# Moving a batched FFT filter's transform between the matmuls of a gated feed-forward block

## The chip, the core and the metric

The kernel runs on one core of one Trainium2 chip. The metric is the device time of one execution in microseconds (us), the median of several runs. The engines spoken of are TensorE (PE, and PEld for its weight loads), VectorE (DVE), ScalarE (ACT), GpSimd (POOL) and SyncE (SP), whose queue issues the DMA transfers. PE writes its results to PSUM, of which there are eight banks of 128 x 512 float32 in this kernel's use; the others work in SBUF.

## What is computed

The input x is 8 batches of 3136 rows by 256 channels, in float32. A filter along the rows is applied by FFT, and a gated feed-forward block of width 1024 with a three-tap convolution along the rows follows.

```python
X = np.fft.rfft(x, axis=1)
y = np.fft.irfft(X * (filt_r + 1j * filt_i), n=3136, axis=1)
h = np.maximum(y @ w_in, 0.0)                     # 256 -> 1024
conv_out = sum(conv_w[k] * shifted(h, k - 1) for k in range(3))
out = (h * sigmoid(conv_out)) @ w_out             # 1024 -> 256
```

## The kernel before

**The transform.** 3136 is 112 x 28. The FFT, the filter and the inverse FFT are done as four stages of matmuls, each over 14 pieces per batch; a piece holds two of 28 columns or groups. Stage 1 (`first`, L323) multiplies x by tables `s1_sb`, and `store` (L313) copies the result from PSUM with ScalarE (L315) and sends it to a buffer `a_dram` in device memory. Stage 2 (`second`, L330) reads that buffer back in another order and multiplies it by `s2_sb`; `filt` (L340) applies the filter with three DVE instructions (L346 to L348) and one POOL sum (L350). Stage 3 (`third`, L353) multiplies by tables `i1_sb`, and `store` sends the result to `b_dram`. Stage 4 (`last_stage`, L210) reads that back and multiplies by `m2_sb`. Its result is the filtered y, written to SBUF by `last_out` (L219) as two tiles, a high part (`hi_act`, L146, ScalarE) and the remainder (`lo_dve`, L149, or `lo_pool`, L152). Because of the two trips through device memory, stage 2 of a batch needs all 14 pieces of its stage 1, and stage 4 all 14 of its stage 3.

**The forward part** (the loop at L375) runs stages 1 to 3 of all eight batches, one piece of each per iteration, with stage 1 some 18 iterations ahead of the rest (`SKEW`, L363). Tables and filter stay in SBUF. Stage 4 of batch 0 comes at its end (L416 to L422). The weights arrive as 64-bit floats and are converted to float32 in small steps by DVE, ACT and POOL (`convert_weights`, L279), also in this loop; PSUM is shared out as five banks under the name ps and three under pp.

**The gated layers** (the loop at L511) are 448 steps m. A step handles 448 rows and 128 of the 1024 hidden channels, in a software pipeline written out by hand: `inner` for step m (six matmuls into one bank `ps_h`), the projection `project` for step m-6 (three matmuls for each of four or three output tiles, into four banks `po`), then `relu` (two ScalarE instructions, L448 and L450) and `conv` (two DVE instructions, L455 and L456) for m-1, `gate` (sigmoid on ScalarE, L460, product on DVE, L461) for m-2, `split_g` (ScalarE and POOL) for m-3, and `evacuate`, which copies a finished `po` to SBUF by DVE (L496) in two of 16 steps. A `ps_h` bank comes free with the product L461. Stage 4 of batches 1 to 7 runs here: the dictionary `pieces` (L503) spreads its 98 pieces over the steps, two to three steps apart, leaving out steps of 16 named in `AVOID`; a piece takes one of the four `ps_h` banks, its matmuls stand between `inner` and `project`, and `last_out` stands near the end of the step. The order on PE, DVE, ACT and POOL is that of the program (`manual_schedule`).

Of the kernel before, what the change touches and what calls it, by code (L numbers as in the profile page):

```python
# [16 lines left out]
S = 3136  # L17
# [107 lines left out]
def tile_fft_filter_gated_ffn(  # L125
# [3 lines left out]
    fr: bass.AP,  # L129
    fi: bass.AP,  # L130
# [52 lines left out]
    b_dram = [dram.tile([N2, 112, D], F32, name=f"b_dram{b}") for b in range(B)]  # L183

    wc = ctx.enter_context(tc.tile_pool(name="wc", bufs=1))
    m2_sb = wc.tile([112, N1], F32, name="m2_sb")
    cw = wc.tile([128, 3, NF], F32, name="cw")
# [3 lines left out]
    wo = [wc.tile([128, NF, D], F32R, name=f"wo{h}") for h in range(2)]  # L191


    ys, yps = {}, []
    lasts = {}

    def last_load(b, c):
        br = lp.tile([112, 2, D], F32, name="br", bufs=4)
        nc.sync.dma_start(out=br, in_=b_dram[b][c:c + 2].rearrange("n p d -> p n d"))
        lasts[b, c] = br  # L200
# [9 lines left out]
    def last_stage(b, c, ps):  # L210

        br = lasts[b, c]
        for j in range(2):
            for k in range(KT):
                o = ps[:, (2 * k + j) * N1:(2 * k + j + 1) * N1]
                nc.tensor.matmul(o, lhsT=br[:, j, 128 * k:128 * k + 128], rhs=m2_sb, start=True, stop=True)  # L216
        lasts[b, c] = ps

    def last_out(b, c):  # L219
        yh, yl = y_slices(b, slice(c, c + 2))  # L220
        pv = lasts.pop((b, c))[:, 0:4 * N1].rearrange("p (k c a) -> p k c a", c=2, a=N1)
        if b == 0:
            v = lp.tile([128, KT, 2, N1], F32, name="v")
            nc.scalar.activation(v, pv, AF.Copy)
            hi_act(yh, pv)
            lo_pool(yl, v, yh)
        else:
            hi_act(yh, pv)
            lo_dve(yl, pv, yh)

    forward_pools = ExitStack()
    xp = forward_pools.enter_context(tc.tile_pool(name="xp", bufs=2, side="right"))
    s1_sb = xp.tile([112, N2, 112], F32, name="s1_sb", bufs=1)
    with (
        tc.tile_pool(name="fc", bufs=1) as fc,
        tc.tile_pool(name="fp", bufs=2) as fp,
        tc.tile_pool(name="fps", bufs=5, space=bass.MemoryType.PSUM) as fps,
    ):
        cv = forward_pools.enter_context(tc.tile_pool(name="cv", bufs=2))
        s2_sb = fc.tile([112, 120], F32, name="s2_sb")  # L240
        s2s_sb = fc.tile([112, 120], F32, name="s2s_sb")
        i1_sb = fc.tile([120, G, 112], F32, name="i1_sb")

        turned = [fc.tile([120, 2, D], F32, name=f"v{k}") for k in range(2)]
        for v in turned:
            nc.gpsimd.memset(v[32:64], 0.0)
        t1_sb = fc.tile([120, G, D], F32, name="t1_sb")
        t2_sb = fc.tile([120, G, D], F32, name="t2_sb")

        rows = {}  # L250

        def load_filter(c):
            for e in (4 * c, 4 * c + 2):
                nc.sync.dma_start(out=t1_sb[0:64, e:e + 2], in_=fr[:, e:e + 2])
                nc.sync.dma_start(out=t2_sb[56:120, e:e + 2], in_=fi[:, e:e + 2])

        def copy_filter(c):
            sl = slice(4 * c, 4 * c + 4)
            nc.scalar.activation(t1_sb[64:120, sl], t1_sb[0:56, sl], AF.Copy)
            nc.scalar.activation(t2_sb[0:56, sl], t2_sb[64:120, sl], AF.Copy)  # L260
            if c == 6:
                nc.sync.dma_start(out=t1_sb[92:93, G - 1], in_=nyq)

        raws = {}

        def load_weights(k):
            raws[k] = raw = cv.tile([128, 2, 512], I32, name="raw")
            for part, src in enumerate((w_in, w_out)):
                nc.sync.dma_start(out=raw[:, part], in_=src[:, 512 * k:512 * k + 512])

        def convert_conv():
            n = 3 * NF
            raw = cv.tile([128, 2, 512], I32, name="raw")
            nc.sync.dma_start(out=raw[:, 0, 0:2 * n], in_=conv_w)
            yield
            em = cv.tile([128, 2, 512], I32, name="em", bufs=1)
            yield from to_f32(cw.rearrange("p k f -> p (k f)"), raw[:, 0, 0:2 * n], em[:, 0, 0:n], em[:, 1, 0:n])

        def convert_weights():  # L279

            for k in range(8):
                raw = raws.pop(k)
                em = cv.tile([128, 2, 512], I32, name="em", bufs=1)
                ws = cv.tile([128, 2, 256], F32, name="ws")
# [12 lines left out]
        NP = 14  # L297
        parts = {}
        psums = {}

        def pool(kind):
            return xp if kind in ("x", "sa") else fp

        def load(kind, b, p):
            r = pool(kind).tile([112, 2, D], F32, name=kind, bufs=8 if kind == "x" else 5)
            if kind == "x":
                v = x[b].rearrange("(p n) d -> p n d", n=N2)
            else:
                v = a_dram[b].rearrange("n (r g) d -> (n r) g d", g=G)
            nc.sync.dma_start(out=r, in_=v[:, 2 * p:2 * p + 2])  # L310
            rows[kind, b, p] = r

        def store(kind, b, p, ps):  # L313
            st = pool(kind).tile([112, 2, D], F32, name=kind, bufs=4)
            nc.scalar.activation(st, ps, AF.Copy)  # L315
            sl = slice(2 * p, 2 * p + 2)
            if kind == "sa":
                v = a_dram[b][sl].rearrange("n p d -> p n d")
            else:
                v = b_dram[b].rearrange("n (r g) d -> (n r) g d", g=G)[:, sl]  # L320
            nc.sync.dma_start(out=v, in_=st)

        def first(b, p):  # L323
            r = rows.pop(("x", b, p))
            ps = fps.tile([112, 2, D], F32, name="ps")
            for j in range(2):
                nc.tensor.matmul(ps[:, j], lhsT=s1_sb[:, 2 * p + j], rhs=r[:, j], start=True, stop=True)  # L327
            return ps

        def second(b, p):  # L330
            r = rows.pop(("a", b, p))
            pp = fps.tile([120, 2, D], F32, name="pp", bufs=3)
            if p < NP - 1:
                nc.tensor.matmul(pp, lhsT=s2_sb, rhs=r, start=True, stop=True)  # L334
            else:
                for j, m in ((0, s2_sb), (1, s2s_sb)):
                    nc.tensor.matmul(pp[:, j], lhsT=m, rhs=r[:, j], start=True, stop=True)
            psums[b, p] = pp

        def filt(b, p):  # L340


            pp, v = psums.pop((b, p)), turned[p % 2]
            sl = slice(2 * p, 2 * p + 2)
            u = fp.tile([120, 2, D], F32, name="u", bufs=3)
            nc.vector.tensor_mul(u, pp, t1_sb[:, sl])  # L346
            nc.vector.tensor_mul(v[64:120], pp[0:56], t2_sb[0:56, sl])
            nc.vector.scalar_tensor_tensor(out=v[0:56], in0=pp[64:120], scalar=-1.0, in1=t2_sb[64:120, sl], op0=ALU.mult, op1=ALU.mult)  # L348
            z = fp.tile([120, 2, D], F32, name="z", bufs=3)
            nc.gpsimd.tensor_tensor(out=z, in0=u, in1=v, op=ALU.add)  # L350
            parts["z", b, p] = z

        def third(b, p):  # L353
            z = parts.pop(("z", b, p))
            ps = fps.tile([112, 2, D], F32, name="ps")
            for j in range(2):
                nc.tensor.matmul(ps[:, j], lhsT=i1_sb[:, 2 * p + j], rhs=z[:, j], start=True, stop=True)  # L357
            return ps

        def at(i):  # L360
            return divmod(i, NP) if 0 <= i < NP * B else None

        SKEW = NP + 4  # L363
        nc.sync.dma_start(out=s1_sb[:, 0:4], in_=s1[:, 0:4])
        load("x", 0, 0)
        load("x", 0, 1)
        for c in range(1, 4):
            nc.sync.dma_start(out=s1_sb[:, 4 * c:4 * c + 4], in_=s1[:, 4 * c:4 * c + 4])
            load("x", 0, 2 * c)
            load("x", 0, 2 * c + 1)  # L370
        csteps, wsteps = convert_conv(), convert_weights()
        done = NP * B + 8
        NI = max(NP * B + SKEW + 5, done + N2 // 2 + 3)
        with tc.manual_schedule(engines=COMPUTE):
            for i in range(NI):  # L375
                f, m = i, i - SKEW
                if i == done:
                    for _ in wsteps:
                        pass
                    forward_pools.close()  # L380
                    yps.append(ctx.enter_context(tc.tile_pool(name="y_even", bufs=1, side="right", reuse_waits="tile")))
                    lp = ctx.enter_context(tc.tile_pool(name="lp", bufs=2, side="right", reuse_waits="tile"))
# [192 lines left out]
```

## Time and profile before

| what | value |
|---|---|
| median of 3 runs | 1564.08 us (1561.53 to 1565.73) |
| span of the profiled execution, first to last instruction | 1562.6 us |
| granted PE clock, mean of that execution | 0.990 |
| DMA traffic over the span | 166.82 MB, mean 107 GB/s |
| stage-4 pieces among the gated layers | 98 |

The profile is of one execution; durations taken from it are set against its own span. What the runs' times hold beyond the span is the start and the end of the program, and the median of the runs is 1.5 us above this span. "Busy" of PE counts pipelined matmuls whose ends are modelled, so prices of PE work are better read from start to start.

### The profile page before, as it was taken

Reading aid. Unit: us, or ns where it says so; the run is one execution under the profiler, and the core shown is the slowest. Engines: PE = TensorE matmul, PEld = TensorE weight load, DVE = VectorE, ACT = ScalarE, POOL = GpSimd, SP = SyncE. Lnnn points to the kernel's source line nnn. Section 1 sums busy time; section 2 is a strip of 40 time slices with the busy share of each in tenths; the row PEclk is TensorE's granted clock in tenths of the full one; section 3 lists DMA queues with packets and bytes.
Section 4 is the critical chain, followed back from the end, with each engine's and each line's share of the span. In section 5 each row is a group of like instructions: output and inputs, shape, how many; then the busy total and the mean of one; then the engine's idle time right before and its main releaser. Section 6 shows DMA issues by size and latency. Waiting matters only on the chain.

```text
span 1562.6 us, 26358 instructions
## 1 busy us (share of the span) xinstructions
PE 1500.9 (96%) x9424; PEld 1345.8 (86%) x9424; DVE 1267.5 (81%) x1951; ACT 1195.0 (76%) x2176; POOL 716.0 (46%) x638
## 2 busy tenths in 40 slices
PE   5689998998999999999999999999999999999998
PEld 3456666657999999999999999999999999999998
DVE  0578888885888888888888888888888888888887
ACT  3444444447888888888888888888888888888887
POOL 0256555666444444444444444444444444444444
PEclk9799999999999999999999999999999999999999
DMA  9999999994111011111110111111011110100001
GB/s 292 289 337 344 340 341 339 341 282 122 31 54 48 30 48 48 49 48 48 48 42 26 35 54 48 48 48 48 31 42 48 49 53 26 48 25 25 24 25 48
DMA packets 129397, 166.82 MB, mean 107 GB/s; under 512 B 10906, under 2 KB 87795, under 8 KB 129267
## 3 DMA queue, kind: packets, MB, share of 16 engines
q1 hardware_dynamic: 129267, 165.14, 33.1%
q8 instruction: 75, 1.23, 0.3%
q14 instruction: 55, 0.45, 0.1%
HBM read 88.03 MB, written 77.07 MB: 106 GB/s over the span
## 4 chain that ended last, share of the span: by engine, by line
PE 84%; DMA 11%; DVE 2%; ACT 1%; SPq 1%; issue 1%; POOL 0%; ACTq 0%; POOLq 0%; DVEq 0%
PE ps_h L178 12%; PE ps_h L179 12%; PE ps_h L177 11%; PE po L481 11%; PE po L483 11%; PE po L482 11%; PE ps_h L216 6%; PE pp L334 3%; DMA a<-a_dram 3%; PE ps L357 3%; DMA b_dram<-sb 3%; PE ps L327 3%; DMA a_dram<-sa 2%; DMA x<-in_x 1%; DMA i_sb<-in_i 1%; ACT y L146 1%
## 5 line engine op out<-in xcount | busy, mean ns | idle before, releaser
L152 POOL TENSOR_TENSOR g<-t,g 128x448 fp32r<-128x448 f32 x448 | 517.5, 1155 | 663.4 <-ACT g L146 259.7
L481 PE MATMUL po<-wo,g 128*128 128x256 f32 x1568 | 441.5, 282 | 0.0
L483 PE MATMUL po<-wo,g 128*128 128x256 f32 x1568 | 433.8, 277 | 0.0
L482 PE MATMUL po<-wo,g 128*128 128x256 f32 x1568 | 433.4, 276 | 0.0
L455 DVE SCALAR_TENSOR_TENSOR t<-ps_h,cw,t 128x448 f32<-128x448 f32 x448 | 305.5, 682 | 92.3 <-ACT t L450 81.7
L178 PE MATMUL ps_h<-y,wi 128*128 128x450 f32 x896 | 330.6, 369 | 4.6 <-DVE y L149 3.9
L177 PE MATMUL ps_h<-y,wi 128*128 128x450 f32 x896 | 329.1, 367 | 4.9 <-ACT y L146 3.2
L179 PE MATMUL ps_h<-y,wi 128*128 128x450 f32 x896 | 329.0, 367 | 0.0
L456 DVE SCALAR_TENSOR_TENSOR t<-ps_h,cw,t 128x448 f32<-128x448 f32 x448 | 306.5, 684 | 16.0
L450 ACT ACTIVATE t<-ps_h,cw 128x448 f32<-128x448 f32 x448 | 284.7, 636 | 41.8 <-ACT ps_h L448 0.7
L481 PEld LDWEIGHTS po<-wo,g 128*128 128x128 f32 x1568 | 294.8, 188 | 7.0
L482 PEld LDWEIGHTS po<-wo,g 128*128 128x128 f32 x1568 | 294.3, 188 | 5.7
L483 PEld LDWEIGHTS po<-wo,g 128*128 128x128 f32 x1568 | 294.5, 188 | 0.0
L448 ACT ACTIVATE ps_h<-ps_h 128x450 f32<-128x450 f32 x448 | 251.8, 562 | 33.0 <-PE ps_h L179 28.3
L461 DVE TENSOR_TENSOR t<-ps_h,t 128x448 f32<-128x448 f32 x448 | 275.1, 614 | 0.1
L460 ACT ACTIVATE t<-t 128x448 f32<-128x448 f32 x448 | 255.0, 569 | 11.9 <-DVE t L456 10.8
L146 ACT ACTIVATE g<-t 128x448 fp32r<-128x448 f32 x448 | 254.6, 568 | 0.2 <-DVE t L461 0.2
L350 POOL TENSOR_TENSOR z<-u,v 120x512 f32<-120x512 f32 x112 | 156.7, 1399 | 155.8 <-DVE v L348 149.5
L177 PEld LDWEIGHTS ps_h<-y,wi 128*128 128x128 f32 x896 | 170.3, 190 | 13.2 <-ACT y L146 4.2
L315 ACT ACTIVATE sb<-ps 112x512 f32<-112x512 f32 x112 | 66.8, 596 | 149.5 <-DMA b_dram<-sb 93.0
L178 PEld LDWEIGHTS ps_h<-y,wi 128*128 128x128 f32 x896 | 168.5, 188 | 13.9 <-DVE y L149 5.9
L179 PEld LDWEIGHTS ps_h<-y,wi 128*128 128x128 f32 x896 | 168.5, 188 | 13.9
(52 smaller groups left out, 1484.6 us busy)
## 6 DMA issues: line engine op xcount, KB each, us to landing
x<-in_x SPq DMA_DIRECT2D x112, 224.0 KB, 4.8
a_dram<-sa SPq DMA_DIRECT2D x112, 224.0 KB, 4.6
a<-a_dram SPq DMA_DIRECT2D x112, 224.0 KB, 4.7
b_dram<-sb SPq DMA_DIRECT2D x112, 224.0 KB, 4.4
br<-b_dram SPq DMA_DIRECT2D x112, 224.0 KB, 2.6
out<-ot SPq DMA_DIRECT2D x27, 896.0 KB, 4.1
raw<-in_w_in SPq DMA_DIRECT2D x8, 256.0 KB, 5.2
raw<-in_w_out SPq DMA_DIRECT2D x8, 256.0 KB, 5.7
```

Of the source, the lines that this page charges most:

```text
L146: nc.scalar.activation(dst, src, AF.Copy)
L152: nc.gpsimd.tensor_tensor(out=dst, in0=src, in1=hi.bitcast(F32), op=ALU.subtract)
L177: nc.tensor.matmul(ps, lhsT=wh, rhs=rh, start=start, stop=False, **kw)
L178: nc.tensor.matmul(ps, lhsT=wh, rhs=rl, start=False, stop=False, **kw)
L179: nc.tensor.matmul(ps, lhsT=wl, rhs=rh, start=False, stop=stop, **kw)
L450: nc.scalar.activation(t, h[:, 1:SUB + 1], AF.Copy, scale=cw[:, 1, f:f + 1])
L455: nc.vector.scalar_tensor_tensor(out=t, in0=h[:, 0:SUB], scalar=cw[:, 0, f:f + 1], in1=t, op0=ALU.mult, op1=ALU.add)
L456: nc.vector.scalar_tensor_tensor(out=t, in0=h[:, 2:SUB + 2], scalar=cw[:, 2, f:f + 1], in1=t, op0=ALU.mult, op1=ALU.add)
L461: nc.vector.tensor_mul(t, h[:, 1:SUB + 1], t)
L481: nc.tensor.matmul(o, lhsT=gh[:, sl], rhs=wo[0][:, f], start=first, stop=False, skip_group_check=True)
L482: nc.tensor.matmul(o, lhsT=gh[:, sl], rhs=wo[1][:, f], start=False, stop=False, skip_group_check=True)
L483: nc.tensor.matmul(o, lhsT=gl[:, sl], rhs=wo[0][:, f], start=False, stop=last, skip_group_check=True)
```

## The change

Only batch 0 goes through all four stages ahead of the gated layers, and with its stage 4 runs stage 1 of batch 1. Every other piece of the transform runs among the gated layers' steps, by a plan written out by a formula. Kinds "1" to "4" are the four stages. For batch t, pieces of kinds "2" and "3" take alternate steps; kind "4" takes the last steps before the layers reach the batch; kind "1" of the next batch takes what is free, twice per step in a few steps.

The tables and the filter no longer stay in SBUF: each piece of kinds "1", "2" and "3" loads what it needs, a few pieces ahead. All pieces go through one bank, `ps_t`; `ps_h` has three banks instead of four, and the split g three buffers instead of four. Output of kind "4" is first copied from PSUM to SBUF by DVE; ScalarE and POOL make the two parts of y from that copy. The output tile `ot` becomes one tile per `po` bank, each sent by itself. The two filter inputs become one array with both parts on 128 rows.

The core of the diff:

```diff
+        for q in range(NP):
+            ps = psum()
+            by_column(ps, tabs["1", q // 2][:, 2 * (q % 2):2 * (q % 2) + 2], rows.pop(("1", q)))
+            store(sp, "1", 1, q, ps, 3, "sa")
...
+            fourth(ps, rows.pop(("4", q)))
+            yh, yl = y_slices(0, pair(q))
+            hi_act(yh, as_y(ps[:, 0:4 * N1]))
+            lo_dve(yl, as_y(ps[:, 0:4 * N1]), yh)
...
-    ps_h = ctx.enter_context(tc.tile_pool(name="ps_h", bufs=4, space=bass.MemoryType.PSUM, reuse_waits="tile"))
+    ps_h = ctx.enter_context(tc.tile_pool(name="ps_h", bufs=3, space=bass.MemoryType.PSUM, reuse_waits="tile"))
+    ps_t = ctx.enter_context(tc.tile_pool(name="ps_t", bufs=1, space=bass.MemoryType.PSUM, reuse_waits="tile"))
...
-            gs[j, f] = [wp.tile([128, 2 * SUB], F32R, name=f"g{h}", bufs=4) for h in range(2)]
+            gs[j, f] = [wp.tile([128, 2 * SUB], F32R, name=f"g{h}", bufs=3) for h in range(2)]
...
+    for t in range(1, B):
+        w, n = (NF * NSUB * (t - 1), 49) if t % 2 else (NF * NSUB * (t - 1) - 7, 63)
+        at2 = 4 if t == 1 else 0 if t % 2 else 10
+        late = range(at2 + 34, n - 1)
+        taken = set()
+        for q in range(NP):
+            at4 = late[q * len(late) // NP]
+            taken |= {at2 + 2 * q, at2 + 3 + 2 * q, at4}
+            put(w + at2 + 2 * q, "2", t, q)
+            put(w + at2 + 3 + 2 * q, "3", t, q)
+            put(w + at4, "4", t, q)
+        free = [s for s in range(n if t % 2 else n - 4) if s not in taken]
...
+    def want_in():
+        while wanted["in"] < min(done["in"] + 5, len(inputs)) and ready(inputs[wanted["in"]]):
...
+            got_in[op] = load_in(tp, *op, 5, "tin")
...
+    def transform(op):
+        kind, b, q = op
+        banks[op] = ps = ps_t.tile([128, 512], F32, name="ps_t")
...
+    def transformed(op):
+        kind, b, q = op
+        ps = banks.pop(op)
+        if kind in "13":
+            store(tp, kind, b, q, ps, 3, "st")
+            stored[kind, b] = stored.get((kind, b), 0) + 1
+        if kind == "2":
+            got_z[b, q] = filt(ps, q, got_filter.pop(op))
+        if kind == "4":
+            v = tp.tile([128, 2, D], F32, name="z", bufs=3).rearrange("p j d -> p (j d)")[:, 0:4 * N1]
+            nc.vector.tensor_copy(v, ps[:, 0:4 * N1])
+            yh, yl = y_slices(b, pair(q))
+            hi_act(yh, as_y(v))
+            lo_pool(yl, as_y(v), yh)
...
             if a := at(m):
                 inner(*a)
-            if m in pieces:
-                last_stage(*pieces[m], ps_h.tile([128, 512], F32, name="ps_h"))
+            for op in ops[0:1]:
+                transform(op)
             if a := at(m - PLAG):
                 project(*a)
...
             if a := at(m - PLAG):
                 evacuate(*a)
+            for n, op in enumerate(ops):
+                if n:
+                    transform(op)
+                transformed(op)
+                want_in()
```

More of the change, by code (lines that the diff above doesn't have):

```diff
@@ L191, in tile_fft_filter_gated_ffn @@
     wo = [wc.tile([128, NF, D], F32R, name=f"wo{h}") for h in range(2)]
[L194 to L200, printed above, removed]
+    turned = [wc.tile([120, 2, D], F32, name=f"v{k}") for k in range(2)]
+    for v in turned:
+        nc.gpsimd.memset(v[32:64], 0.0)
+    tp = ctx.enter_context(tc.tile_pool(name="tp", bufs=2))
+    yps = [ctx.enter_context(tc.tile_pool(name="y_even", bufs=1, side="right"))]
+    ys = {}
     def y_slices(b, sl):
@@ L231, in tile_fft_filter_gated_ffn, with as_y @@
-    forward_pools = ExitStack()
-    xp = forward_pools.enter_context(tc.tile_pool(name="xp", bufs=2, side="right"))
-    s1_sb = xp.tile([112, N2, 112], F32, name="s1_sb", bufs=1)
+    def as_y(p):
+        return p.rearrange("p (k c a) -> p k c a", c=2, a=N1)
     with (
-        tc.tile_pool(name="fc", bufs=1) as fc,
-        tc.tile_pool(name="fp", bufs=2) as fp,
-        tc.tile_pool(name="fps", bufs=5, space=bass.MemoryType.PSUM) as fps,
-    ):
[L239 to L264, printed above, removed]
@@ L295, in convert_weights @@
                     load_weights(k + 2)
[L297 to L366, printed above, removed]
@@ new lines, in table, with load_filter @@
+        def table(kind, c):
+            k, src = {"1": (112, s1), "3": (120, i1)}[kind]
+            tabs[kind, c] = t = sp.tile([120, 4, 112], F32, name=f"tab{kind}", bufs=3)[0:k]
+            nc.sync.dma_start(out=t, in_=src[:, 4 * c:4 * c + 4])
+        def load_filter(q):
+            fts[q] = f = sp.tile([120, 2, 2, D], F32, name="f", bufs=4)
+            nc.sync.dma_start(out=f[0:64, :, 0], in_=filt_in[0:64, pair(q), 0])
+            nc.sync.dma_start(out=f[56:120, :, 1], in_=filt_in[56:120, pair(q), 1])
@@ new lines, in a_load @@
+        def a_load(q):
+            rows["2", q] = load_in(sp, "2", 0, q, 5, "a")
+        for c in range(3):
+            table("1", c)
+            x_load(2 * c)
+            x_load(2 * c + 1)
+        nc.sync.dma_start(out=s2_sb, in_=s2[:, 0:120])
+        nc.sync.dma_start(out=s2s_sb, in_=s2s[:, 0:120])
+        nc.sync.dma_start(out=m2_sb, in_=m2)
+        for q in range(NP):
+            ps = psum()
+            by_column(ps, tabs["1", q // 2][:, 2 * (q % 2):2 * (q % 2) + 2], rows.pop(("1", q)))
+            store(sp, "1", 0, q, ps, 3, "sa")
+            if q % 2 and q // 2 + 3 < 7:
+                table("1", q // 2 + 3)
+            if q + 6 < NP:
+                x_load(q + 6)
+            next(csteps, None)
+            if q in (4, 6, 8, 10):
+                load_filter((q - 4) // 2)
+            if q == 9:
+                load_weights(0)
+                load_weights(1)
+            if q in (5, 7, 9):
+                table("3", (q - 5) // 2)
@@ new lines, in tile_fft_filter_gated_ffn @@
+        for q in range(4):
+            copy_filter(q)
+        for q in range(5):
+            a_load(q)
+        pss = {}
+        for i in range(NP + 4):
+            if i < NP:
+                pss[i] = psum()
+                second(pss[i], i, rows.pop(("2", i)))
+            if 0 <= i - 3 < NP:
+                q = i - 3
+                ps = psum()
+                by_column(ps, tabs["3", q // 2][:, 2 * (q % 2):2 * (q % 2) + 2], zs.pop(q))
+                store(sp, "3", 0, q, ps, 3, "sb")
+                if q % 2 and q // 2 + 3 < 7:
+                    table("3", q // 2 + 3)
+            if 0 <= i - 1 < NP:
+                zs[i - 1] = filt(pss.pop(i - 1), i - 1, fts.pop(i - 1))
+                if i + 3 < NP:
+                    load_filter(i + 3)
+            if 4 <= i + 2 < NP:
+                copy_filter(i + 2)
+            if i + 5 < NP:
+                a_load(i + 5)
+            for _ in range(4):
+                next(wsteps, None)
@@ L496, in evacuate @@
                 nc.vector.tensor_copy(o, src)
-            if end:
-                nc.sync.dma_start(out=outv[j][:, 2 * k:2 * k + n], in_=ot[:, 2 * k:2 * k + n])
-        if i == 1 and not end:
-            nc.sync.dma_start(out=outv[j], in_=ot)
+            nc.sync.dma_start(out=outv[j][:, 2 * k:2 * k + n], in_=ot[:, 0:n])
     NH = 16 * (B * S // CH)
-    pieces = {}
-    for b in range(1, B):
-        start = ((NSUB * (b - 1) - 1) // 2 + 1) * 16 + (4 if b == 1 else 0)
-        stop = NSUB * b // 2 * 16 + NSUB * b % 2
-        free = [m for m in range(start, stop) if m % 16 not in AVOID]
-        for c in range(N2 // 2):
-            pieces[free[c * (len(free) - 1) // (N2 // 2 - 1)]] = (b, 2 * c)
+    plan = {}
@@ new lines, in put @@
+    def put(m, kind, b, q):
+        plan.setdefault(m, []).append((kind, b, q))
+    early = {}
+    for t in range(1, B):
[3 more added lines that the diff above has]
+        taken = set()
+        for q in range(NP):
+            at4 = late[q * len(late) // NP]
[4 more added lines that the diff above has]
+        free = [s for s in range(n if t % 2 else n - 4) if s not in taken]
+        for q in range(early.get(t, NP), NP):
+            put(w + free.pop(0), "1", t, q)
+        if t + 1 < B:
+            early[t + 1] = min(NP, len(free))
+            if not t % 2:
+                free = sorted(free + free[:NP - len(free)])
+                early[t + 1] = NP
+            for q, s in enumerate(free[:NP]):
+                put(w + s, "1", t + 1, q)
@@ new lines, in tile_fft_filter_gated_ffn, with ready @@
+    order = [(m, op) for m in sorted(plan) for op in plan[m]]
+    inputs = [op for _, op in order if op[0] in "124"]
+    tables = [op for _, op in order if op[0] in "13"]
+    filters = [op for _, op in order if op[0] == "2"]
+    got_in, got_table, got_filter, got_z, banks = {}, {}, {}, {}, {}
+    stored = {("1", 1): NP}
+    def ready(op):
+        kind, b, _ = op
+        return kind == "1" or stored.get(({"2": "1", "4": "3"}[kind], b), 0) == NP
+    def want_in():
+        while wanted["in"] < min(done["in"] + 5, len(inputs)) and ready(inputs[wanted["in"]]):
+            op = inputs[wanted["in"]]
+            wanted["in"] += 1
+            got_in[op] = load_in(tp, *op, 5, "tin")
@@ new lines, in want_table, with want_filter @@
+    def want_table(n):
+        for op in tables[n:n + 1]:
+            k, src = {"1": (112, s1), "3": (120, i1)}[op[0]]
+            got_table[op] = t = tp.tile([120, 2, 112], F32, name="tab", bufs=4)[0:k]
+            nc.sync.dma_start(out=t, in_=src[:, pair(op[2])])
+    def want_filter(n):
+        for op in filters[n:n + 1]:
+            got_filter[op] = f = tp.tile([128, 2, 2, D], F32, name="filt")
+            nc.sync.dma_start(out=f, in_=filt_in[:, pair(op[2])])
+    done, wanted = {"in": 0, "table": 0, "filter": 0}, {"in": 0}
@@ new lines, in tile_fft_filter_gated_ffn @@
+    want_in()
+    for n in range(3):
+        want_table(n)
+    want_filter(0)
+    def transform(op):
+        kind, b, q = op
+        banks[op] = ps = ps_t.tile([128, 512], F32, name="ps_t")
+        if kind in "124":
+            done["in"] += 1
+            r = got_in.pop(op)
+        if kind in "13":
+            want_table(done["table"] + 3)
+            done["table"] += 1
+            w = got_table.pop(op)
+        if kind == "1":
+            by_column(ps, w, r)
+        if kind == "2":
+            want_filter(done["filter"] + 1)
+            done["filter"] += 1
+            second(ps, q, r)
+        if kind == "3":
+            by_column(ps, w, got_z.pop((b, q)))
+        if kind == "4":
+            fourth(ps, r)
```

186 lines of the change are left out of this document (93 added, 93 removed).

## The prediction

> **What bounds the kernel now.** I read the page's busy table and slices first, then the chain, then busy time in stretches.
>
> ```profile
> span 1562.6 us, 26358 instructions
> PE 1500.9 (96%) x9424; PEld 1345.8 (86%) x9424; DVE 1267.5 (81%) x1951; ACT 1195.0 (76%) x2176; POOL 716.0 (46%) x638
> PE   5689998998999999999999999999999999999998
> DMA  9999999994111011111110111111011110100001
> PE 84%; DMA 11%; DVE 2%; ACT 1%; SPq 1%; issue 1%; POOL 0%; ACTq 0%; POOLq 0%; DVEq 0%
> ```
>
> The slices split the kernel in two. For nine slices the DMA row stands at 9; then it falls to 1 and PE stays at 9 to the end. The stretches give the numbers (columns: PE, PEld, DVE, ACT, POOL busy us with instruction counts, granted clock, DMA share, GB/s), and the timeline gives the border, the first matmul of the gated layers:
>
> ```profile
> 0.00:39.00 39.00, 22.25 (x76) 14.08 (x76) 1.17 (x7) 13.63 (x21) 1.51 (x8) 0.94 0.97 292
> 234.00:273.00 39.00, 34.64 (x134) 23.26 (x134) 31.97 (x49) 16.46 (x29) 21.44 (x16) 1.00 1.01 339
> 375.00:1562.00 1187.00, 1177.94 (x8175) 1130.03 (x8175) 1004.51 (x1552) 1023.61 (x1892) 518.45 (x476) 1.00 0.13 41
> 373.39 0.74 PE L177 MATMUL ps_h<-y,wi 128*128 128x450 f32 x1 [3.18 <-ACT y L146]
> ```
>
> So the transform of all batches takes 373.4 us at a DMA share of 1.0, and the gated layers take 1562.6 - 373.4 = 1189 us with PE busy 99% of it. The point that decides the change: PE isn't idle in the first part either. It is busy 34.6 of 39 us there. Moving the transform behind the border takes out little idle PE time.
>
> PE's price of a step comes from starts on the PE timeline:
>
> ```profile
> 902.18 0.37 PE L177 MATMUL ps_h<-y,wi 128*128 128x450 f32 x1
> 903.41 1.04 PE L216 MATMUL ps_h<-m_sb,br 112*128 112x112 f32 x8
> 905.68 0.37 PE L177 MATMUL ps_h<-y,wi 128*128 128x450 f32 x1
> 907.92 0.37 PE L177 MATMUL ps_h<-y,wi 128*128 128x450 f32 x1
> 910.51 0.37 PE L177 MATMUL ps_h<-y,wi 128*128 128x450 f32 x1
> ```
>
> Steps with four and with three projection tiles alternate: 2.59 us (907.92 to 910.51) and 2.24 (905.68 to 907.92), mean 2.42. The four-tile step with a piece takes 3.50, so a transform piece costs 3.50 - 2.59 = **0.91 us** of PE. Check: 448 x 2.42 + 98 x 0.91 = 1173 of the 1189; 16 us are the fill and the drain.
>
> **The change, part by part.** The new plan puts 98 pieces each of kinds 2, 3 and 4 and 84 of kind 1 between the steps: 378, of which 98 (kind 4) were there already. Kinds 1 and 3 are four half-matmuls and kind 2 is two of double width; the row of 289.33 below shows four in 1.03 us, so they get the same 0.91.
>
> (1) PE work added behind the border: 280 x 0.91 = 255 us. With the old 1189 that is **1444 us** if nothing waits.
>
> (2) What stays ahead: batch 0's four stages and batch 1's first. Rows for it (the chain; the issue table; groups by form):
>
> ```profile
> 42.87 2.08 PE pp L334 x2
> b_dram<-sb SPq DMA_DIRECT2D x112, 224.0 KB, 4.4
> br<-b_dram SPq DMA_DIRECT2D x112, 224.0 KB, 2.6
> L164 DVE TENSOR_TENSOR em<-em 128x512 int32<-128x512 int32 x8 | 5.5, 692 | 0.2
> L160 DVE TENSOR_SCALAR em<-raw 128x512 int32<-128x512 int32 x8 | 3.4, 427 | 0.2
> 219.29 0.69 DVE L346 TENSOR_TENSOR u<-pp,t_sb 120x512 f32<-120x512 f32 x1 [0.46 <-PE pp L334]
> 221.45 0.43 DVE L160 TENSOR_SCALAR em<-raw 128x512 int32<-128x512 int32 x1
> ```
>
> Stage 1: the old kernel reaches its first second-stage matmul at 42.9 us, having moved about 292 GB/s x 39 us = 11.4 MB. The new order queues about 10.7 MB ahead of that point (14 inputs, 14 stores, tables, four filters, two weight chunks), so I take 41 us. Stages 2 and 3 have nothing beside them now except the weight conversion, and DVE has to do both: 14 filters x 2.16 us (219.29 to 221.45) = 30, and 72 of the 88 conversion steps of 3 x 5.5 + 4 x 3.4 = 30 us, so 25. Together 55, more than their 13 MB of DMA (28 rows of 224 KB, ten filters of 256 KB, four tables, six weight chunks of 512 KB: 38 us at 340 GB/s). The last store and the first reload cost 4.4 + 2.6 us, and the first x loads are queued behind six other transfers: some 9 us. Then 14 rounds that each move 0.79 MB (an x, a store, a reload, half a table): 11 MB at 340 GB/s, 32 us; the last output adds 2. Sum 41 + 55 + 9 + 32 + 2 = **139 us**, bounds 128 and 152. Against 373.4, 234 us go; against them stand 255. Even without one new wait the change costs about 20 us: the serial stretch of one batch leaves PE idle as long (139 - 70 x 0.91 = 75 us) as the old pipelined stretch of eight did, and longer (373.4 - 350 x 0.91 = 55 us; 350 pieces are three kinds of 112 and fourteen of kind 4).
>
> (3) The new waits. Engines run their queues in the order written, and the old trace shows it: ScalarE does the piece's output, then the next step's relu (ACT, DVE timelines; the last rows are the copy of po by its two widths).
>
> ```profile
> 904.49 1.05 ACT L146 ACTIVATE y<-ps_h 128x448 fp32r<-128x448 f32 x1 [0.79 <-PE ps_h L216]
> 905.30 0.67 ACT L448 ACTIVATE ps_h<-ps_h 128x450 f32<-128x450 f32 x1
> 906.07 0.64 ACT L450 ACTIVATE t<-ps_h,cw 128x448 f32<-128x448 f32 x1
> 906.74 0.68 DVE L455 SCALAR_TENSOR_TENSOR t<-ps_h,cw,t 128x448 f32<-128x448 f32 x1
> 908.06 0.61 DVE L461 TENSOR_TENSOR t<-ps_h,t 128x448 f32<-128x448 f32 x1
> L496 DVE COPY ot<-po 128x512 f32<-128x512 f32 x83 | 54.2, 679 | 3.2 <-PE po L483 3.2
> L496 DVE COPY ot<-po 128x256 f32<-128x256 f32 x27 | 11.2, 413 | 0.0
> ```
>
> *Kind 4.* Before, the output y was read by ScalarE straight from PSUM, so nothing ahead of it was DVE's. Now DVE copies the bank to v, and ScalarE reads v. That closes a ring, once per step, when kind-4 pieces stand in neighbouring steps: copy (DVE, 0.61 for 448 elements by the two widths) -> y (ACT) -> relu -> scaled copy -> both convolution steps -> product (DVE) -> next copy, queued behind that product. From the rows: y start to convolution start 2.25, to the product's end 908.67 another 1.93, copy 0.61: **4.8 us**, where PE needs 2.42 + 0.91 = 3.33. The matmuls wait because three ps_h banks let a step start only when the product three steps back is done. Writing the plan out by the diff's formula: batches 3, 5, 7 have 14 kind-4 steps in a row, batches 2, 4, 6 runs of 3 to 4 with single gaps, batch 1 ten steps of which four hold two pieces. Ninety single steps x 1.47 = 132; four doubles (another 1.12 for the matmuls, 0.61 copy) x 2.34 = 9; less, by estimate, 1.1 at each of seven run starts (there the copy waits for its own matmuls only, 2.3 us after the step's start) and 0.4 at nine gaps: 130. Nine of these steps also evacuate po ahead of the copy (1.36 or 1.09 us, mean 1.23): 11. **141 us.** Unknown here is y from SBUF: the strided write (L146, 1.05) makes me keep its 0.81 start to start; the same copy to a contiguous g starts its successor 0.47 later, which would save 34.
>
> *Kinds 2 and 3* alternate for 28 to 31 steps per batch through one bank. Ring of two steps: third-stage matmuls -> store copy (ACT) -> relu -> scaled copy -> convolution, product -> filter (DVE) -> bank free.
>
> ```profile
> 289.33 1.03 PE L357 MATMUL ps<-z,i_sb 120*112 120x256 f32 x4
> 290.45 0.60 ACT L315 ACTIVATE sb<-ps 112x512 f32<-112x512 f32 x1 [1.13 <-PE ps L357]
> 907.53 0.53 ACT L448 ACTIVATE ps_h<-ps_h 128x450 f32<-128x450 f32 x1
> 908.83 0.68 DVE L455 SCALAR_TENSOR_TENSOR t<-ps_h,cw,t 128x448 f32<-128x448 f32 x1 [0.16 <-ACT t L450]
> ```
>
> 1.12 + 0.55 to 0.60 + 1.30 + 1.9 + 2.16 = 7.1 us against PE's 2 x 3.33 = 6.65: 98 x 0.45 = 44. In 13 of the kind-2 steps po is evacuated ahead of the filter, 13 x 1.23 = 16, and 2 for the kind-3 ones: **62 us**, bounds 20 and 75.
>
> *ps_h from four to three banks* elsewhere: eleven pairs of evacuating steps lose an estimated 0.7 us each: two steps, 4.84, less 1.23 for the matmuls, 1.30 for relu and scaled copy and 1.93 for convolution and product, leave 0.4 of slack, and an evacuation takes 1.23: **8 us**. g from four buffers to three is 0: the projection of the pair three back is done before the split that reuses it.
>
> DMA costs 0: four pieces move six rows of 224 KB, a filter of 512 KB and two tables of about 100 KB, 2.1 MB, so with the output about 0.58 MB per step of 3.3 us, 175 GB/s, half of the 339 above, and inputs are called five pieces ahead. If that cover were gone, a landing of 4 to 5 us would add one step's wait each. SP's queue holds a store's wait for ACT ahead of the next loads; the same five pieces hide it. POOL gets 98 sums and 98 differences, 516 us to about 790 of 1650: no bound.
>
> Sum: 139 + 1444 + 141 + 62 + 8 = **1794 us** of span; the run's time lies about 1.5 us above the span (median 1564.08 beside 1562.6): 1795. Ends: 128 + 1444 + 96 + 20 = 1688, and 152 + 1454 + 170 + 75 + 8 = about 1860.
>
> **The rivals.** *Clock.* New short PE waits could lower the granted clock:
>
> ```profile
> 64.00:70.00 6.00, 4.43 (x16) 2.51 (x15) 4.07 (x8) 2.96 (x4) 3.09 (x2) 1.00 1.05 301
> 372.00:378.00 6.00, 3.92 (x10) 3.12 (x11) 0.00 (x0) 2.20 (x4) 2.54 (x2) 0.54 0.09 30
> ```
>
> After one wait of 3.2 us the clock was 0.54; with PE 74% busy in shorter gaps it was 1.00. The kind-4 runs would have PE at 70% with gaps of 1.5 us. If the clock fell to 0.54 in them, a step would take 3.33 / 0.54 = 6.2 us, 1.4 more on 94 steps: 1795 + 130 = about 1925. By the Trainium skill, TensorE: Matmul & The Clock Gate, section "A second HAM failure mode: psum-queue depth-cycling", frequent micro-idles between matmul groups that cycle PSUM banks do make the clock swing. The row at 64 us speaks against it for gaps of this length.
>
> *No ring binds*: the buffers take up all waits, as PE's 99% in the old trace shows for pieces standing alone: 139 + 1444 + 1.5 = 1585. The spacing speaks against it: the old pieces stand two or three steps apart, the new ones in neighbouring steps.
>
> *Faster*: the stretch ahead turns out DMA-bound throughout, with the DVE work hidden and no turnaround: 41 + 38 + 32 = 111, and pieces fill 5 us of the layers' start; with no ring, 111 + 1439 + 1.5 = 1552. It decides at a stretch ahead of 119 us (1563 - 1444). DVE's 55 us speaks against it.
>
> *The change doesn't do what it says*: its order is written out by hand, and the old trace runs as written. I give this nothing of its own.
>
> **How the numbers follow.** Rings as priced 0.80; clock 0.05; no ring 0.06; faster 0.04; rings bind in part (1600 to 1660) 0.05. The range runs from 1660, past the lower bound towards the partial case, to 1850, and leaves out the other three and the tail above. What this measurement can tell from no change is about 0.3%, 5 us. Faster 0.04, within 0.01, slower 0.95.
>
> **What would show it.** First gated-layer matmul near 139 us; in a run of kind-4 steps, L177 groups about 4.8 us apart instead of 3.3, PE waiting on the DVE product, ACT's y on the DVE copy, DVE's convolution on the ACT scaled copy; pairs of kinds 2 and 3 about 7.1 us; after the last piece, steps of 2.42 as now. I am wrong if the first matmul comes before 119 us, if kind-4 steps run at 3.3, or if PE waits for DMA.

## The result, and the profile after

The changed kernel takes 1822.7 us (median of four runs, 1820.8 to 1827.5) against 1564.8: a ratio of 1.166, 95% interval 1.164 to 1.168. The profiled execution has a span of 1821.9 us. Its page, with the same lines as before:

```profile
span 1821.9 us, 27328 instructions
PE 1586.1 (87%) x9424; PEld 1380.1 (76%) x9424; DVE 1242.6 (68%) x1965; ACT 1179.6 (65%) x2176; POOL 819.7 (45%) x722
PE   4658998899887999799998899889998889978998
DMA  9767553475421554155552355326553245210001
```

PE has the same 9424 instructions and is no longer full, but no other engine is fuller than it was: DVE fell from 81% to 68%, ACT from 76% to 65%, and the DMA row lies at half. No engine is full over the span, so the engines wait for one another. The waits (engine and line that waited, what released it; us in total, times, longest) name the partners; L433 is the first convolution step, L428 the scaled copy, L439 the product, L572 the copy of a kind-4 piece, L145 ScalarE's y:

```profile
DVE t L433 <- ACT t L428: 455.7, 314, 4.0
ACT y L145 <- DVE z L572: 169.6, 98, 3.5
PEld ps_h L176 <- DVE t L439: 139.8, 108, 3.6
PE ps_h L176 <- DVE t L439: 116.9, 104, 3.4
```

In the kernel before, the first of them (there L455 for L450) was 81.7 us. The ring (the chain of work that comes back to the engine where it began, so that each turn of it must wait for the one before) is visible in one turn, a kind-4 step of batch 3 (timelines of DVE, ACT and PE):

```profile
741.06 0.61 DVE L572 COPY z<-ps_t 128x448 f32<-128x448 f32 x1
741.71 1.05 ACT L145 ACTIVATE y<-z 128x448 fp32r<-128x448 f32 x1 [1.60 <-DVE z L572]
742.55 0.64 ACT L426 ACTIVATE ps_h<-ps_h 128x450 f32<-128x450 f32 x1
743.29 0.64 ACT L428 ACTIVATE t<-ps_h,cw 128x448 f32<-128x448 f32 x1
743.96 0.68 DVE L433 SCALAR_TENSOR_TENSOR t<-ps_h,cw,t 128x448 f32<-128x448 f32 x1 [2.29 <-ACT t L428]
745.28 0.61 DVE L439 TENSOR_TENSOR t<-ps_h,t 128x448 f32<-128x448 f32 x1
745.81 0.61 DVE L572 COPY z<-ps_t 128x448 f32<-128x448 f32 x1
745.95 0.48 PE L176 MATMUL ps_h<-y,wi 128*128 128x450 f32 x1 [0.96 <-DVE t L439]
```

Each row follows the one above, by its data or in its engine's queue; the second convolution step, between L433 and L439, is left out. From copy to copy it is 4.75 us, and PE's next step waits for the product. In the last stretch of kinds 2 and 3, third-stage matmuls on the chain of waits return every 7.11 us on average:

```profile
1490.57 1.09 PE ps_t L231 x4
...
1533.25 1.09 PE ps_t L231 x4
```

(Seven rows, six pairs in 42.68 us.) The gated layers begin later than forecast:

```profile
152.51 0.44 PE L176 MATMUL ps_h<-y,wi 128*128 128x450 f32 x1 [1.16 <-ACT y L145]
```

To see where time went I took, for each kernel, the starts of the first L176 matmul of steps 8 to 447, and subtracted the forecast's PE prices (2.42 per step, 0.91 per piece). What remains is lost time, sorted by the pieces of the stretch (the steps just behind a run of pieces are counted with it):

| kernel | layers begin, us | lost in kind-4 runs | lost in kinds 2 and 3 | median time |
|---|---|---|---|---|
| changed | 152.5 | 149 | 77 | 1822.7 |
| relu ahead | 151.3 | 6 | 47 | 1647.9 |
| y one step later | 152.0 | 4 | 77 | 1678.4 |
| y from PSUM | 152.9 | 32 | 78 | 1707.9 |
| fewer conversions | 156.5 | 150 | 79 | 1831.5 |
| copy twice | 154.0 | 223 | 76 | 1898.5 |
| relu, evacuation, conversions | 155.4 | 1 | 30 | 1628.5 |
| relu ahead, copy twice | 153.6 | 22 | 51 | 1669.3 |

For the changed kernel 6 us more are lost elsewhere. 152.5 + 149 + 77 + 6 are 384.5 of the span of 1821.9; the other 1437 us are the matmuls at the forecast's prices, fill and drain, so they are what is left and not a second measurement. The prices are borne out where no ring binds: with y one step later, the kind-4 steps of batch 3 take 3.15 and 3.49 us in turn, mean 3.32 against the price of 3.33.

### The profile page after: what moved, and what is told of

It reads as the page before. It is cut to its first block, busy times and chain, and to the rows that moved or that the text cites. A ratio compares the mean times of both kernels' runs of the same rounds, so it can differ in the third digit from the quotient of the medians.

```text
span 1821.9 us, 27328 instructions
## 1 busy us (share of the span) xinstructions
PE 1586.1 (87%) x9424; PEld 1380.1 (76%) x9424; DVE 1242.6 (68%) x1965; ACT 1179.6 (65%) x2176; POOL 819.7 (45%) x722
## 5 line engine op out<-in xcount | busy, mean ns | idle before, releaser
L433 DVE SCALAR_TENSOR_TENSOR t<-ps_h,cw,t 128x448 f32<-128x448 f32 x448 | 306.0, 683 | 459.7 <-ACT t L428 455.7
L459 PE MATMUL po<-wo,g 128*128 128x256 f32 x1568 | 517.9, 330 | 0.0
L176 PE MATMUL ps_h<-y,wi 128*128 128x450 f32 x896 | 345.0, 385 | 118.5 <-DVE t L439 116.9
L460 PE MATMUL po<-wo,g 128*128 128x256 f32 x1568 | 440.0, 281 | 0.0
L461 PE MATMUL po<-wo,g 128*128 128x256 f32 x1568 | 439.3, 280 | 0.0
L177 PE MATMUL ps_h<-y,wi 128*128 128x450 f32 x896 | 331.2, 370 | 0.6 <-DVE y L148 0.6
L178 PE MATMUL ps_h<-y,wi 128*128 128x450 f32 x896 | 329.3, 368 | 0.0
L459 PEld LDWEIGHTS po<-wo,g 128*128 128x128 f32 x1568 | 298.6, 190 | 31.0 <-issue 22.4
L460 PEld LDWEIGHTS po<-wo,g 128*128 128x128 f32 x1568 | 298.6, 190 | 27.7 <-issue 21.7
L428 ACT ACTIVATE t<-ps_h,cw 128x448 f32<-128x448 f32 x448 | 285.0, 636 | 42.0 <-ACT ps_h L426 0.7
L226 ACT ACTIVATE st<-ps_t 112x512 f32<-112x512 f32 x182 | 108.9, 598 | 299.0 <-PE ps_t L231 299.0
L461 PEld LDWEIGHTS po<-wo,g 128*128 128x128 f32 x1568 | 298.6, 190 | 0.0
L176 PEld LDWEIGHTS ps_h<-y,wi 128*128 128x128 f32 x896 | 169.3, 189 | 149.3 <-DVE t L439 139.8
L439 DVE TENSOR_TENSOR t<-ps_h,t 128x448 f32<-128x448 f32 x448 | 275.1, 614 | 0.1
L247 POOL TENSOR_TENSOR z<-z,v 120x512 f32<-120x512 f32 x112 | 146.3, 1306 | 266.4 <-DVE v L246 266.4
L145 ACT ACTIVATE g<-t 128x448 fp32r<-128x448 f32 x448 | 253.7, 566 | 0.1
L145 ACT ACTIVATE y<-z 128x448 fp32r<-128x448 f32 x98 | 104.5, 1066 | 169.6 <-DVE z L572 169.6
L151 POOL TENSOR_TENSOR y<-z,y 128x448 fp32r<-128x448 f32 x98 | 137.6, 1404 | 158.3 <-ACT y L145 158.3
```

The source lines that it names most:

```text
L145: nc.scalar.activation(dst, src, AF.Copy)
L151: nc.gpsimd.tensor_tensor(out=dst, in0=src, in1=hi.bitcast(F32), op=ALU.subtract)
L176: nc.tensor.matmul(ps, lhsT=wh, rhs=rh, start=start, stop=False, **kw)
L177: nc.tensor.matmul(ps, lhsT=wh, rhs=rl, start=False, stop=False, **kw)
L178: nc.tensor.matmul(ps, lhsT=wl, rhs=rh, start=False, stop=stop, **kw)
L428: nc.scalar.activation(t, h[:, 1:SUB + 1], AF.Copy, scale=cw[:, 1, f:f + 1])
```

## The experiments

The theory: two rings through in-order queues. The rivals: the single bank `ps_t`, the added transfers, the fourth `ps_h` bank.

**Relu ahead of the transform's output.** Nothing is removed; two ScalarE instructions change places with the output of the same step.

```diff
             if a := at(m - 1):
-                relu(*a)
                 conv(*a)
...
                 evacuate(*a)
+            if a := at(m):
+                relu(*a)
             for n, op in enumerate(ops):
```

> All pieces, banks, copies and transfers of the changed kernel stay; only the two relu instructions of a step stand ahead of that step's transform output on ScalarE instead of behind it. Ring theory (both rings run through ScalarE's output, then relu, then DVE): steps of kind 4 in a row fall from 4.76 to 3.3-3.5 us, pairs of kinds 2 and 3 from 7.1 to 6.7, in all about 1610 us (1590 to 1645). Single-bank theory (a piece waits because the one before it still holds the one bank, whatever stands behind on ScalarE): no change, 1822 within 15. DMA theory (the reloaded tables and filters): no change either.

1647.9 us, ratio to the kernel before 1.052 (1.049 to 1.055): 175 us gone by an order, and 3 us past the end of the expected range. Steps 151 and 160 of the same kind-4 run now start 29.74 us apart, 3.30 a step, where the changed kernel took 43.10 (4.79). PE timelines, the changed kernel first:

```profile
736.45 0.47 PE L176 MATMUL ps_h<-y,wi 128*128 128x450 f32 x1 [1.63 <-DVE t L439]
...
779.55 0.48 PE L176 MATMUL ps_h<-y,wi 128*128 128x450 f32 x1 [1.30 <-DVE t L439]
```

```profile
672.41 0.36 PE L176 MATMUL ps_h<-y,wi 128*128 128x450 f32 x1
...
702.15 0.36 PE L176 MATMUL ps_h<-y,wi 128*128 128x450 f32 x1
```

The bank and the transfers are the same, so neither is the main cause. The 47 us left in kinds 2 and 3 show on the chain of waits of this kernel: an evacuation of po, then the filter, then the third-stage matmuls that wait for the bank.

```profile
1329.55 0.69 DVE ot L475
1330.24 0.60 DVE z L244
1330.85 0.68 DVE v L245
1331.55 0.70 DVE v L246
1332.39 1.09 PE ps_t L231 x4
```

**Kind 4 alone, by time.** ScalarE's and POOL's split of y goes to the end of the next step; DVE's copy stays.

```diff
-            yh, yl = y_slices(b, pair(q))
-            hi_act(yh, as_y(v))
-            lo_pool(yl, as_y(v), yh)
+            late_y.append((b, q, v))
...
                 evacuate(*a)
+            split_y()
             for n, op in enumerate(ops):
```

> Only kind 4's two instructions that split y (ScalarE, POOL) move, to the end of the next step; DVE's copy stays where it is and empties the bank as before. Ring theory: kind-4 steps 3.3-3.5 us, kinds 2 and 3 untouched at 7.1 a pair, about 1822 - 149 + 10 = 1680 us (1665 to 1700). Single-bank theory: no change, 1822 within 15.

1678.4 us (one run). The kind-4 loss falls from 149 to 4 and the other stays at 77: the two rings are separate.

**Kind 4 alone, by source.** ScalarE reads PSUM, DVE makes the low part.

```diff
-            nc.vector.tensor_copy(v, ps[:, 0:4 * N1])
...
-            hi_act(yh, as_y(v))
-            lo_pool(yl, as_y(v), yh)
+            hi_act(yh, as_y(ps[:, 0:4 * N1]))
+            lo_dve(yl, as_y(ps[:, 0:4 * N1]), yh)
```

> Kind 4 without DVE's copy: ScalarE reads y from PSUM and DVE makes the low part, as in the kernel before. The bank is held some 2.1 us instead of 0.6. Ring theory: no DVE step stands ahead of ScalarE's y any more, kind-4 steps 3.3-3.5, about 1690 us (1670 to 1710). Single-bank theory: the longer hold makes it worse, 90 steps by up to 1 us, about 1880 to 1910.

1707.9 us (one run). The longer hold of the bank does cost something, 32 us against 4 (weight loads of kind-4 matmuls wait 37 times for the low part, 19.3 us together), but it is far better than the copy: what hurt was DVE ahead of ScalarE.

**Filter transfers twice.** A second copy of the `dma_start` in `want_filter`.

> Each of the 98 filter transfers of 512 KB is issued twice into the same tile. Ring theory: the transfers are hidden, 1822 to 1830 us. DMA theory: each doubled transfer adds about 1.7 us where it is waited for (512 KB at 300 GB/s), up to 1990 us.

1823.2 us (one run): 98 transfers of 512 KB more, and no change. The added traffic is hidden.

**Copy twice**, in the changed kernel and in the one with relu ahead (a second copy of the `tensor_copy` line).

> The changed kernel with DVE's copy of a kind-4 piece done twice. Ring theory: each copy is in the ring, 98 x 0.55 to 0.61 = 54 to 60 us more, 1874 to 1884 us, kind-4 steps 5.3 us. Rival (DVE is 68% busy and would hide it): 1822 to 1830.

> The first experiment's order (relu ahead of the transform's output, 1648 us) with DVE's copy of a kind-4 piece done twice, which cost the changed kernel 76 us. Ring theory: with the ring open the second copy fits beside PE, 1648 to 1660 us. Rival (DVE's time itself is what kind 4 waits for): about 1700 or more.

1898.5 us (one run), 76 more and above the expected range. The kind-4 loss rises by 74, which is 0.75 us a copy, more than its own 0.61: a step in the ring goes from 4.75 to 5.38 us, and the steps just behind a run, which wait for the ring as well, rise by as much. With the ring open, 1669.3 us (one run), the second copy costs 21, above the 12 expected, so some of it is still exposed, but not 76.

**Fewer conversions beside batch 0's stages 2 and 3.**

```diff
-            for _ in range(4):
+            for _ in range(2):
                 next(wsteps, None)
```

> The changed kernel with two conversion steps per round instead of four beside batch 0's stages 2 and 3; the rest of the conversion then falls beside stage 4. DVE theory (DVE's filter and conversion bound that stretch): 36 steps x 0.36 us go, the first matmul of the gated layers comes at 138 to 144 us instead of 152.5, and the time falls by as much, to 1808 to 1815 us. Rival (that stretch is bound by transfers and by the waits for the filter's rows): first matmul at 150 or later, 1822 within 4.

1831.5 us; the layers begin at 156.5. Both theories miss. The stretch that the experiment aimed at did shorten by the 13 us: the last stage-3 copy on ScalarE (the changed kernel's row first, then this one's):

```profile
109.57 0.58 ACT L226 ACTIVATE sb<-ps 112x512 f32<-112x512 f32 x1
```

```profile
96.79 0.60 ACT L226 ACTIVATE sb<-ps 112x512 f32<-112x512 f32 x1 [0.21 <-ACT wo L145]
```

It was given back beside stage 4. There the displaced conversion steps stand in ScalarE's queue ahead of the stores and of y. That this is what gave it back was not tried; it is read from waits that grew (41 to 160 us, changed kernel, then this one):

```profile
DVE y L148 <- ACT y L145: 20.6, 13, 7.8
ACT wi L145 <- POOL ws L173: 18.7, 7, 4.7
```

```profile
ACT wi L145 <- POOL ws L173: 29.9, 6, 5.7
DVE y L148 <- ACT y L145: 27.5, 10, 10.0
```

**The three together with the evacuation moved.** Relu ahead as above; the copies of po behind the transform's output, with four buffers; two conversion steps per round.

```diff
+            if a := at(m):
+                relu(*a)
             for n, op in enumerate(ops):
...
                 want_in()
+            if a := at(m - PLAG):
+                evacuate(*a)
```

> Relu ahead of the transform's output as in the first experiment; the copies of po stand behind the transform's output on DVE instead of ahead of it, with a fourth output buffer; two conversion steps per round as above. What is left in the stretches of kinds 2 and 3 after the first experiment is 47 us; the thirteen steps of 5.0 to 5.5 us behind an evacuation would lose 1.8 each (23), the two of 8.4 some 5 each (10 to 13), and the stretch ahead 10: about 1648 - 45 = 1603 us (1595 to 1615). It stays slower than the kernel before, because the stretch ahead and the moved matmuls alone are 142 + 1444 = 1586. Rival (the filter's own hold of the bank is what is left): 1630 to 1640.

1628.5 us, ratio 1.041 (1.039 to 1.042): between the two forecasts, close to the rival's. The loss in kinds 2 and 3 fell from 47 to 30, but the evacuation's part did not all go. With relu ahead alone, each of the thirteen steps behind an evacuation loses 1.9 us or more; here each still loses 1.1 to 1.2, 15 of the 30. Other kind-3 steps lose at most some 0.4. The conversions cost 4 instead of saving 10. This is the best version of the new plan that ran, and it is slower than the kernel before.

**The old plan with the new banks**: three for `ps_h`, one for the pieces.

```diff
-    ps_h = ctx.enter_context(tc.tile_pool(name="ps_h", bufs=4, space=bass.MemoryType.PSUM, reuse_waits="tile"))
+    ps_h = ctx.enter_context(tc.tile_pool(name="ps_h", bufs=3, space=bass.MemoryType.PSUM, reuse_waits="tile"))
+    ps_t = ctx.enter_context(tc.tile_pool(name="ps_t", bufs=1, space=bass.MemoryType.PSUM, reuse_waits="tile"))
...
-                last_stage(*pieces[m], ps_h.tile([128, 512], F32, name="ps_h"))
+                last_stage(*pieces[m], ps_t.tile([128, 512], F32, name="ps_t"))
```

> The kernel before with three ps_h banks and its 98 pieces in a bank of their own, nothing else. The prediction's estimate of 0.7 us per pair of steps that evacuate po would be 28 x 0.7 = 20 us here, 1580 to 1588 us. Rival: the fourth bank was only for the pieces, so within 3 us of the kernel before.

1676.5 us, ratio 1.071 (1.069 to 1.074), 112 more, far outside both. PE waits for the product here too:

```profile
PEld ps_h L177 <- DVE t L462: 98.1, 122, 2.3
PE ps_h L177 <- DVE t L462: 73.6, 121, 2.0
```

So I asked whether this is the number of banks or again the order, and let a piece's output follow one step later (except the last of a batch, and where the next step has a piece too):

```diff
-            if m in pieces:
+            if pieces.get(m - 1) in lasts and m not in pieces:
+                last_out(*pieces[m - 1])
+            if m in pieces and pieces[m][1] == N2 - 2:
                 last_out(*pieces[m])
```

> The old plan with three ps_h banks and a bank for the pieces, as before (1676 us), but a piece's output (ScalarE's high part, DVE's low part) stands one step later, behind that step's product, so that it no longer delays the relu and the convolution of its own step. Order theory (three banks are too few only because the output stands ahead of relu and convolution and lengthens the step's way to the product): 1570 to 1600 us. Rival (three banks are too few for this pipeline in any order): 1650 to 1680.

1595.9 us, ratio 1.019 (1.015 to 1.024): 80 of the 112 were the order, about 30 remain. Set step by step against the kernel before, the old order with the new banks loses 72 us in the steps right behind a piece, and the later output loses nothing there. Its own loss, 26 us in all, lies behind the 28 pairs of steps that evacuate po: 0.9 a pair, where 0.7 was forecast. So a step with an output between its matmuls and its relu needs the fourth bank. In the new plan the pairs that fall in steps without a piece lose 0.9 to 1.6 us, and those beside kind-1 pieces 0 to 0.6: there a step takes PE 3.33 us instead of 2.42, which leaves the product time to arrive.

**The new output in the old plan**: kind 4's copy by DVE, split by ScalarE and POOL, with the old spacing and four shared banks.

```diff
-            hi_act(yh, pv)
-            lo_dve(yl, pv, yh)
+            nc.vector.tensor_copy(v, pv)
+            hi_act(yh, v)
+        lo_pool(yl, v, yh)
```

> The kernel before, plan and four shared banks unchanged, with kind 4's new output: DVE copies the piece, ScalarE and POOL split the copy. Pieces stand two or more steps apart. Ring theory (the copy costs only where kind-4 pieces follow each other step by step): 1563 to 1575 us. Rival (the copy costs its length wherever it is): 98 x 0.6 us more, about 1625.

1660.8 us, ratio 1.061 (1.058 to 1.064): far outside both. The old pieces stand in groups, two or three steps apart, with longer gaps between the groups. Set step by step against the kernel before, about 75 of the 95 us lie in steps with a piece, but not in all of these. Of the 24 pieces that stand seven or more steps behind the last one, 17 lose 0.1 us at most in their own step; the other seven, three steps behind an evacuation of po, lose 0.6 on average. The 71 pieces two or three steps behind another one lose 1.0 on average. So a copy that stands alone, away from an evacuation, costs nothing, as the ring theory has it, but a neighbour still counts at two and three steps, and that the expectation had wrong. One row of the waits, and the rows of the first piece of a group and of the next one, two steps on (timelines of PE, DVE and ACT):

```profile
PEld ps_h L216 <- DVE t L461: 71.2, 80, 1.3
```

```profile
1095.97 1.04 PE L216 MATMUL ps_h<-m_sb,br 112*128 112x112 f32 x8
1097.75 0.62 DVE L227 COPY v<-ps_h 128x448 f32<-128x448 f32 x1
1098.40 1.08 ACT L146 ACTIVATE y<-v 128x448 fp32r<-128x448 f32 x1 [1.61 <-DVE v L227]
1100.67 0.68 DVE L455 SCALAR_TENSOR_TENSOR t<-ps_h,cw,t 128x448 f32<-128x448 f32 x1 [2.31 <-ACT t L450]
1101.99 0.61 DVE L461 TENSOR_TENSOR t<-ps_h,t 128x448 f32<-128x448 f32 x1
1102.66 1.15 PE L216 MATMUL ps_h<-m_sb,br 112*128 112x112 f32 x8 [0.69 <-DVE t L461]
```

The first piece doesn't wait. Its copy puts off ScalarE's y, the relu and scaled copy behind that, and with them the convolution and the product. Two steps later that product still holds the bank, one of the four shared ones, that the next piece needs. A piece that comes later finds the delay made up.

## Why the prediction was right

**PE isn't idle ahead, so moving matmuls gains nothing.** Right. The account leaves 1437 us for matmuls, fill and drain, where 1444 were forecast; it uses the forecast's prices, which the 3.15 and 3.49 us of the kind-4 steps without a ring bear out. With both rings relieved, the new plan is still 64 us behind the kernel before (1628.5 against 1564.6).

**The stretch ahead: 139 us forecast, 152.5 measured.** The terms of stages 1 to 3 were too small: 41 + 55 should have ended them at 96 us, and the last copy starts at 109.6. Some 4 us came late already, since DVE's first filter starts at 45.6. The rest is DVE's. It is the bound that the forecast took it for, busy 59.6 of the 65 us from 45 to 110 (columns as in the stretches before), and the conversions experiment, which took steps of DVE, ScalarE and POOL out of this stretch, shortened it by the 13 us that it should.

```profile
45.00:110.00 65.00, 41.28 (x89) 20.63 (x87) 59.59 (x83) 23.74 (x46) 37.17 (x31) 0.74 0.65 194
```

What the sum left out is that DVE's conversion steps stretch beside POOL. The timelines of POOL and DVE:

```profile
47.83 1.76 POOL L247 TENSOR_TENSOR z<-z,v 120x512 f32<-120x512 f32 x1 [33.69 <-DVE v L246]
48.51 1.37 DVE L169 TENSOR_SCALAR em<-ws 128x512 int32<-128x512 int32 x1
52.80 0.43 DVE L159 TENSOR_SCALAR em<-raw 128x512 int32<-128x512 int32 x1
```

The same kind of instruction takes 0.43 us when it starts just before POOL's sum (the next one starts at 52.84), and 1.37 when it starts inside it; it then ends some 0.3 us after the sum does (POOL's spans are rough). Over all eight it averages 663 ns, and its counterpart in the kernel before 426, where one conversion step followed each filter and started ahead of POOL's sum; here four follow (groups by form, the changed kernel, then the one before; busy us, mean ns):

```profile
L169 DVE TENSOR_SCALAR em<-ws 128x512 int32<-128x512 int32 x8 | 5.3, 663 | 0.3
```

```profile
L170 DVE TENSOR_SCALAR em<-ws 128x512 int32<-128x512 int32 x8 | 3.4, 426 | 0.2
```

Of DVE's 56 instructions of this conversion, 15 are stretched, and these are the ones that start inside an instruction of POOL; they take 9.9 us more than they do elsewhere, 9.5 of them before 110 us. With the late start that makes up the 13. DVE's filter instructions, which read one input from PSUM, keep 0.68 to 0.69 us, and 21 of the 42 start inside an instruction of POOL.

The Trainium skill, SBUF — State Buffer, section "SBUF: two separate sides", says that VectorE and GpSimd share a pair of ports as an exclusive lock, which goes for the whole instruction to the one that starts first, and which VectorE needs in a mode that uses two ports or, beside a GpSimd instruction that reads SBUF, with two inputs in SBUF. This trace agrees, 0.9 us for this instruction. ScalarE's waits for the filter's rows (26.2 us from 41 to 160) can't have cost DVE, which uses these rows, more than the 5.4 us that it idled from 45 to 110.

**Kind 4: 141 forecast, 149 measured**, and 4.75 us per turn against 4.8. The mechanism is shown by three experiments that open the ring at different places. Mis-sized within it is what the ends of a run save. The slack at the start is there: batch 3's run begins with steps of 3.55 and 4.13 us, 1.8 below the turn. But the step behind the run waits for the ring too, 4.77 us where 3.33 would do, so 0.4 of it is left, and not 1.1. Where the step behind has no piece, it takes 4.8 instead of 2.4, and nothing is left.

**Kinds 2 and 3: 62 forecast, 77 measured.** The pair's 7.1 was right (7.11), so the 44 us hold. The rest was mis-sized: I had 18 for evacuations ahead of the filter, and 33 came. Ten of the thirteen steps behind such an evacuation lose 1.9 to 2.0 us. The other three take 7.8 to 8.9 us; before the longest, DVE's fourth output copy waits for one of only three output buffers, a wait that comes five times and to 5.0 us in all, so that it is a part of the excess:

```profile
484.82 0.42 DVE L475 COPY ot<-po 128x256 f32<-128x256 f32 x1 [1.59 <-DMA out<-ot]
485.21 0.69 DVE L244 TENSOR_TENSOR z<-ps_t,filt 120x512 f32<-120x512 f32 x1
```

I had looked at SP's queue and the inputs, not at the output tile that the change split up.

**The fourth `ps_h` bank: 8 forecast, 6 measured here.** That the size came out is luck in part: the forecast had 0.7 us for each of eleven pairs, and a pair lost 0.9 to 1.6 or next to nothing by what stood beside it. The reason given was thin, for the same banks cost the old plan 112 us. Three are too few where steps are short and an output stands ahead of relu.

**DMA at nothing** holds for the loads (1823.2 with the filters sent twice); the waits for an output buffer above are the exception.

**The sum.** 1794 was forecast for the span, and it was 1821.9. The terms don't owe this to errors that cancel: the stretch ahead, kind 4, and kinds 2 and 3 were 13, 8 and 15 us too small, matmuls and banks 7 and 2 too large.

**The rivals.** The clock stayed near full: 0.99 over the gated layers, and 1.00 in a stretch of kind-4 steps with PE busy 60.2 of 74 us (columns as in the stretches before). It was not untouched, though. In the gated layers it fell to half nine times, for 3.4 us each, three of them in the three long steps of kinds 2 and 3, and a kind-4 stretch with two more (batch 2's, 507.4 to 588.3) had 0.96. Where the second copy lengthened the wait in each step to 1.95 us, batch 3's run had 0.89. The changed kernel twice, then copy twice:

```profile
152.50:1807.78 1655.28, 1485.48 (x9037) 1310.86 (x9037) 1154.06 (x1838) 1113.22 (x2064) 769.33 (x668) 0.99 0.41 122
1383.00:1457.00 74.00, 60.24 (x407) 55.24 (x406) 40.56 (x68) 48.99 (x82) 37.97 (x35) 1.00 0.27 81
```

```profile
739.00:820.00 81.00, 62.10 (x368) 55.97 (x367) 46.78 (x77) 45.44 (x77) 36.80 (x33) 0.89 0.20 60
```

The forecast's rival, 0.54 through all kind-4 runs, did not come. "No ring" would have been 1585; with the rings open and the evacuation moved the plan reaches 1628.5, of which 16 are the longer stretch ahead and 30 what kinds 2 and 3 still lose. "Faster" needed the layers to begin by 119 us; no kernel of the new plan began them before 151.

## What to carry to other kernels

Before moving work into a full engine's stretch, count the idle time of that engine where the work is now; if it has none, nothing can be gained there. Then follow one step's output through every in-order queue until it comes back to the engine where it began, and divide the length of that ring by the steps that it spans: 4.8 us against 3.33 was readable from rows of the old trace, though neither of its engines ended above 70% busy. The turns need not stand side by side: in the old plan a product put off by one piece still held up the next piece two or three steps on. Where a ring binds, try first to change the place of two instructions in a queue; here that alone gave back 175 us.

## What was not expected of the hardware

A DVE instruction from SBUF to SBUF took 1.37 us instead of 0.43 when it started inside a POOL sum, while DVE's filter instructions, which read PSUM, kept their 0.69. Dropping a stretch's DVE work by 13 us moved its end by 13 us and the end of the next not at all (it came 4 us later): as far as the waits show, the work that was put off then stood in another in-order queue, ahead of what that stretch had to deliver.
